# Attention of the first two batches turned on TensorE, first loads in a fixed order on two queues, folded weights of the second batch from slices that are still on the chip

## The chip, the cores and the metric

The kernel runs on one core of a Trainium2 chip. The metric is device time in microseconds (us): the median of the runs of the program, of which there are three for the kernel before. A profiled execution of the same program gives the trace; its own time is told beside its span. TensorE is called PE in the rows (its weight loads PEld), VectorE is DVE, ScalarE is ACT, GpSimd is POOL, SyncE is SP.

## The reference

For 8 batches of 8 heads, 576 tokens and a head size of 64, with 32 memory slots per head:

```
a    = softmax(phi over the tokens)            # phi: 576 x 32 per head
k_m  = a^T k ; v_m = a^T v                     # 32 x 64 per head
attn = softmax(q k_m^T / sqrt(64)) v_m         # per token over 32 slots
x    = attn with the heads side by side        # 4608 tokens x 512
out  = relu(x w_in)^2 w_out                    # 512 -> 2048 -> 512
```

w_in and w_out come as 64-bit floats; q, k, v and phi as 32-bit floats.

## The kernel before

**Folding.** The kernel never forms x. For each batch it multiplies v_m into w_in once (the folded weights, tile `vw`, 2048 columns in 8 slices of 256) and then multiplies the attention weights (tile `ath` and its rest `atl`) with `vw`. Every product of 32-bit accuracy is made of three products of a high and a low part, which is why tiles come in pairs (`ath`/`atl`, `gh`/`glo`, `VTh`/`VTl`).

**Stages.** `memory(b, hh)` (hh is one half of the heads) takes the softmax of phi (tiles `phi`, `mx`, `mc`, `pmx`) and multiplies it with k and v (tile `pkv`, lines L426 and L439). `scores` and `attention` turn q by blocks of 32x32 on VectorE (L546), multiply it with the block-diagonal k_m (`kb`, L539; product L551), turn the scores back on VectorE (L555), take the softmax over slots (L563 to L570) and turn the result once more on VectorE (L585) into `ath` and `atl`. `piece` and `decode` load a slice of w_in or w_out as 64-bit words (`raw`, L322) and make two 32-bit parts of it on VectorE, ScalarE and partly TensorE (L324 to L357); for w_out slices from the third on, the last sum is an accumulating DMA from POOL (L361). `vw_alone` folds a slice for the first two batches (L493, L501), `vw_step` for the others. `step(g)` is one batch times one block of 128 of the 2048 columns: `mm1` (L622, relu and square), `mm2` (L652, L653, L655 into the four banks `acc`). There are 128 such steps.

**Order.** Batch 0 takes the first 8 column blocks, then batch 1 those 8 and the other 8, then batch 0 its other 8; the batches behind come one by one. Every decoded w_in slice is written to DRAM (L364, two DMAs of 256 KB per half slice, from POOL) and read again later (`wi_again`, L369): for slices 0 to 3 already for the second batch, for all slices again for batches 2 to 7.

**Who sets the order.** The code only records operations with their reads and writes. `Plan.order` then lists them by planned costs and due times and issues each engine's instructions in that one order; an engine carries out its list strictly in order, so whatever stands behind a waiting instruction waits with it. Nearly all loads are issued by SP.

Of the kernel before, what the change touches and what calls it, by code (L numbers as in the profile page):

```python
# [26 lines left out]
LANDS = {"SP": 1400, "POOL": 4000}  # L27
# [179 lines left out]
def tile_attention_moe(  # L207
# [54 lines left out]
    def dma(fn, size, r=(), w=(), eng="SP", two=False, **more):  # L262
        e = {"SP": nc.sync, "POOL": nc.gpsimd}[eng]
        issue = 700 if eng == "POOL" else 1250 if two else 620
        return op({eng: issue}, lambda _: fn(e.dma_start), r=r, w=w, size=size, lat=0, **more)
# [19 lines left out]


# [9 lines left out]
    w_in_parts = []  # L296
    for x in ("hi", "lo"):
        t = dram.tile([DM, FF], F32, name=f"w_in_{x}")
        w_in_parts.append(plan.buf(f"w_in_{x}", lambda _, t=t: t))
    wi = {}  # L300
    wo = {}

    def wi_rows(x, s, hh):

        return w_in_parts[x]()[2 * hh * P:(2 * hh + 2) * P, s * SL:(s + 1) * SL].rearrange("(c p) f -> p c f", p=P)

    def decode(kind, j, h, room):
# [14 lines left out]
        dma(lambda d: d(R().rearrange("p (c f t) -> p c f t", c=src.shape[1], t=2), src), 4096 * P, w=[rk], lead=True)  # L322
# [6 lines left out]
        if kind == "wi":  # L329
            t = wi[0, j, 0, h] = st([P, 2, 2, SL], F32R, "wi", f"wi0_{j}_{h}", 3)  # L330
# [31 lines left out]
        if kind == "wi":  # L362
            for x in (0, 1):
                dma(lambda d, x=x: d(wi_rows(x, j, h), t()[:, x].bitcast(F32)), 2048 * P, r=[(t, (h, x))], w=[(w_in_parts[x], (j, h))], eng="POOL", lead=True)  # L364

    def wi_again(n, s, hh):
        t = wi[n, s, 1, hh] = st([P, 2, 2, SL], F32R, "wi", f"wi{n}_{s}_{hh}", 3)
        for x in (0, 1):
            dma(lambda d, x=x: d(t()[:, x].bitcast(F32), wi_rows(x, s, hh)), 2048 * P, r=[(w_in_parts[x], (s, hh))], w=[(t, (hh, x))], lead=True)  # L369
# [22 lines left out]
    def memory(b, hh, where=None):  # L392
# [5 lines left out]
        dma(lambda d: tokens(d, a(), phi[b, 4 * hh:4 * hh + 4]), 4 * S * M * 4, [], [(A, "in")], two=True, lead=True)  # L398
        KV = []
        for x in (0, 1):  # L400
            t = st([P, 4 * SC * D], F32, where[x] if where else "KV", f"KV{u}_{x}", 1 if where else 2)
            kv = lambda t=t: t().rearrange("p (i h c d) -> p i h c d", i=2, h=2, c=SC)
            for i, src in ((0, k), (1, v)):
                dma(lambda d, i=i, src=src, kv=kv, x=x: tokens(d, kv()[:, i], src[b, 4 * hh + 2 * x:4 * hh + 2 * x + 2]),
                    2 * S * D * 4, [], [(t, i)], two=True, lead=True)
# [28 lines left out]
        def sums(e):  # L434
# [49 lines left out]
    def vw_alone(s, bp):  # L484

        ts_ = [wi[0, s, bp if s < 4 else 0, hh] for hh in (0, 1)]
# [17 lines left out]
    def vw_step(n, s, hh):  # L504
        t = wi[n, s, 1, hh]
# [22 lines left out]
    def scores(b, hh, split):  # L528
# [284 lines left out]
```

## Time and profile before

| | |
|---|---|
| three runs | 831.05 us median, 829.07 to 832.75 |
| the profiled execution | 829.28 us, of which the span is 827.6 us |
| granted TensorE clock, mean over the span | 0.983 of 2.4 GHz |
| TensorE busy | 777.8 us, 94% of the span |
| VectorE busy | 547.2 us, 66% |
| ScalarE busy | 396.4 us, 48% |
| moved by DMA | 101.05 MB |

The busy share of TensorE is an average over stages that differ: in the first 60 us it is idle for 24 us, from 250 us to 810 us for 2 us. The span has to be read stage by stage. Matmuls are pipelined and their ends are modelled, so a busy TensorE is not always one at its peak; where its granted clock is 0.5 it is at 1.2 GHz, otherwise at 2.4 GHz.

### The profile page before, as it was taken

How to read it: one execution, taken by the hardware profiler on the slowest of the kernel's cores; microseconds unless marked ns; L12 is line 12 of the kernel's file. 1: busy time of each engine (PE TensorE's matmuls, PEld its weight loads, DVE VectorE, ACT ScalarE, POOL GpSimd, SP SyncE). 2: the span in 40 equal slices, each digit the busy share in tenths (PEclk: the TensorE clock that was granted, in tenths of full speed). 3: DMA queues.
4: the chain of work that ended last, by engine and by line, in shares of the span. 5: the costliest groups of instructions: out<-in, count | busy, mean ns of one | idle time of the engine just before them, and what ended most of it. 6: DMA issues, size and time to landing. Idle time of an engine off the chain costs nothing.

```text
span 827.6 us, 13055 instructions
## 1 busy us (share of the span) xinstructions
PE 777.8 (94%) x4820; PEld 650.1 (79%) x4820; DVE 547.2 (66%) x1224; ACT 396.4 (48%) x904; POOL 65.1 (8%) x103
## 2 busy tenths in 40 slices
PE   4679998899979999999999999999999999999995
PEld 2346887788868788888788888888788888888883
DVE  3888997484447856786768465786778555874540
ACT  1456676476535355554436355453434355543220
POOL 3112211221100100001000100010000100000000
PEclk9999999899999999999999999999999999999998
DMA  7978956566455543322562433413512433100001
GB/s 213 292 223 274 264 162 180 158 186 187 112 147 165 146 129 103 102 55 54 141 171 58 126 115 103 124 38 96 140 45 79 130 109 97 40 19 33 1 1 63
DMA packets 92804, 101.05 MB, mean 122 GB/s; under 512 B 24836, under 2 KB 78084, under 8 KB 92740
## 3 DMA queue, kind: packets, MB, share of 16 engines
q1 hardware_dynamic: 80292, 81.55, 34.1%
q0 software_dynamic: 12448, 18.66, 9.3%
q8 instruction: 38, 0.62, 0.3%
q14 instruction: 26, 0.21, 0.1%
HBM read 79.17 MB, written 17.83 MB: 117 GB/s over the span
## 4 chain that ended last, share of the span: by engine, by line
PE 69%; DVE 11%; DMA 9%; issue 4%; ACT 4%; SPq 1%; POOL 1%; DVEq 0%; ACTq 0%; POOLq 0%
PE h L622 19%; PE acc L655 12%; PE acc L652 11%; PE acc L653 11%; PE accl L678 5%; PE pvw L513 4%; DMA raw<-in_moe_w_in_dram 3%; PE psc L551 2%; PE pkv L426 2%; DMA wo<-work 2%; DMA phi<-in_phi_dram 2%; ACT vw L260 1%; DMA q<-in_q_dram 1%; DMA raw<-in_moe_w_out_dram 1%; DVE glo L632 1%
## 5 line engine op out<-in xcount | busy, mean ns | idle before, releaser
L622 PE MATMUL h<-ath,vw 128*128 128x320 f32 (+1 forms) x1024 | 211.9, 299 | 1.5 <-DVE ath L260 1.3
L652 PE MATMUL acc<-wo,gh 128*128 128x512 f32 x512 | 206.8, 404 | 0.6 <-ACT gh L628 0.4
L653 PE MATMUL acc<-wo,gh 128*128 128x512 f32 x512 | 202.1, 395 | 0.0
L622 PEld LDWEIGHTS h<-ath,vw 128*128 128x128 f32 x1024 | 172.1, 190 | 18.2 <-DVE ath L260 1.9
L655 PE MATMUL acc<-wo,glo 128*128 128x512 f32 x512 | 163.7, 412 | 3.5 <-DVE glo L632 3.3
L260 ACT CAST vw<-pvw 64x256 fp32r<-64x256 f32 (+1 forms) x224 | 85.8, 397 | 94.5 <-PE pvw L513 47.1
L522 DVE TENSOR_TENSOR vw<-pvw,vw 64x256 fp32r<-64x256 f32 x192 | 78.7, 420 | 73.5 <-ACT vw L260 71.7
L652 PEld LDWEIGHTS acc<-wo,gh 128*128 128x128 f32 x512 | 96.8, 189 | 21.0 <-issue 2.2
L622 PE MATMUL h<-atl,vw 128*128 128x320 f32 (+1 forms) x512 | 110.7, 296 | 0.2
L655 PEld LDWEIGHTS acc<-wo,glo 128*128 128x128 f32 x512 | 91.0, 191 | 24.1 <-DVE glo L632 10.1
L653 PEld LDWEIGHTS acc<-wo,gh 128*128 128x128 f32 x512 | 96.8, 189 | 16.5
L628 ACT ACTIVATE gh<-r 128x512 fp32r<-128x512 f32 x128 | 80.7, 630 | 41.8 <-DVE r L627 30.4
L632 DVE TENSOR_TENSOR glo<-r,gh 128x512 fp32r<-128x512 f32 x128 | 87.5, 684 | 12.1 <-ACT r L630 10.0
L626 ACT ACTIVATE r<-h 128x256 f32<-128x256 f32 (+1 forms) x146 | 58.8, 405 | 64.9 <-PE h L622 63.8
L627 DVE TENSOR_SCALAR r<-h 128x320 f32<-128x320 f32 (+1 forms) x110 | 50.3, 459 | 56.3 <-PE h L622 55.7
L622 PEld LDWEIGHTS h<-atl,vw 128*128 128x128 f32 x512 | 83.1, 191 | 1.2 <-DVE atl L589 0.8
L630 ACT ACTIVATE r<-r 128x576 f32<-128x576 f32 x99 | 67.8, 685 | 2.4
L629 ACT ACTIVATE gl<-r 128x64 fp32r<-128x64 f32 x128 | 32.6, 255 | 64.1 <-DVE r L627 62.1
L678 PE MATMUL accl<-wo,gl 128*128 128x512 f32 x192 | 52.3, 396 | 0.1
L678 PEld LDWEIGHTS accl<-wo,gl 128*128 128x128 f32 x192 | 34.9, 188 | 7.3 <-DVE o L260 0.5
L551 PE MATMUL psc<-qT,kb 128*128 128x256 f32 (+1 forms) x128 | 37.8, 415 | 1.6 <-DVE S L555 1.4
L513 PE MATMUL pvw<-wi,VTh 128*128 128x256 f32 x192 | 37.6, 288 | 0.3 <-DVE vw L522 0.3
(107 smaller groups left out, 836.0 us busy)
## 6 DMA issues: line engine op xcount, KB each, us to landing
wi<-w_in_hi SPq DMA_DIRECT2D x56, 256.0 KB
wi<-w_in_lo SPq DMA_DIRECT2D x56, 256.0 KB
q<-in_q_dram SPq DMA_DIRECT2D x32, 288.0 KB
KV<-in_k_dram SPq DMA_DIRECT2D x32, 256.0 KB
KV<-in_v_dram SPq DMA_DIRECT2D x32, 256.0 KB
raw<-in_moe_w_in_dram SPq DMA_DIRECT2D x16, 512.0 KB
raw<-in_moe_w_out_dram SPq DMA_DIRECT2D x16, 512.0 KB
out_dram<-o POOLq DMA_DIRECT2D x20, 256.0 KB, 8.3
```

Source lines behind the costliest of these rows:

```text
L260: nc.scalar.copy(o, i) if e == "ACT" else ENG[e].tensor_copy(o, i)
L513: nc.tensor.matmul(pw()[:, x * SL:(x + 1) * SL], l()[:, 2 * hh + x, :], w(r, x), start=(i == 0), stop=(i == 2))
L522: vec({"DVE": tt(SL)}, lambda e, V=V, pr=pr, src=src: nc.vector.tensor_sub(V()[pr, 1, hh, :], src(), V()[pr, 0, hh, :].bitcast(F32)), [pw, ...
L622: nc.tensor.matmul(p()[:, 0:n], V()[:, l, hh, c0:c0 + P], x()[:, hh, cs], start=(i == 0), stop=(i == 5))
L626: op({"ACT": act(n) - 30, **({} if b < 2 else {"DVE": tt(n)})}, lambda e, cs=cs, n=n, p=p: nc.scalar.activation(r()[:, cs], p()[:, 0:n], A ...
L628: op({"ACT": act(SM)}, lambda e: nc.scalar.activation(gh(), r()[:, 0:SM], AF.Square), [r], [gh])
L630: op({"ACT": act(S), **({} if b < 2 else {"DVE": tt(S)})}, lambda e: nc.scalar.activation(r(), r(), AF.Square) if e == "ACT" else nc.vecto ...
L632: vec({"DVE": tt(SM)}, lambda e: nc.vector.tensor_sub(glo(), r()[:, 0:SM], gh().bitcast(F32)), [r, gh], [glo])
L652: nc.tensor.matmul(a(), gh()[:, c], t()[:, 0], start=f0, stop=False)
L653: nc.tensor.matmul(a(), gh()[:, c], t()[:, 1], start=False, stop=False)
L655: nc.tensor.matmul(a(), glo()[:, c], t()[:, 0], start=False, stop=f1)
L678: nc.tensor.matmul(a(), G()[:, l, :], t()[:, w], start=(ff == 0 and n == 0), stop=(ff == NFF - 1 and n == 2))
```

## The change

1. **First loads.** `dma` may take a name out of a list `FIRST`. Such a load may be issued by SP or by ACT, whichever is free by the plan, and the list fixes the order.
2. **Attention of batches 0 and 1** is a function of its own. q is loaded in natural order (64 values of a token at a time, 256 bytes), turned by TensorE (`turn`, four transposes of 128x128 into a bank), copied by ScalarE, multiplied token block by token block (`psc`: 8 matmuls of 128x64 per half instead of 4 of 128x256 and 128x320), and the softmax result is turned by TensorE again (`back`). k_m and v_m leave `memory` by one pair of TensorE transposes. The 32x32 transposes of VectorE for these two batches are gone; batches 2 to 7 keep them.
3. **The second batch's folded weights.** Slices 0 and 1 of w_in stay in tiles of their own (`W4a` to `W5b`) until batch 1 has used them; slices 2 and 3 are folded for batch 1 directly behind batch 0. The second batch's 16 reads of 256 KB (L369, slices 0 to 3) are gone. `memory(1, *)` and `attention(1)` stand earlier in the program.
4. **The stored slices** lie in DRAM as one tensor in the order of the tile: one DMA of 512 KB per half slice in place of two, for the writes and for the reads that stay (batches 2 to 7).

```diff
-    def dma(fn, size, r=(), w=(), eng="SP", two=False, **more):
-        e = {"SP": nc.sync, "POOL": nc.gpsimd}[eng]
+    def dma(fn, size, r=(), w=(), eng="SP", two=False, first=None, **more):
+        q_ = {"SP": nc.sync, "ACT": nc.scalar, "POOL": nc.gpsimd}
         issue = 700 if eng == "POOL" else 1250 if two else 620
+        ways = {eng: issue}
+        if first in FIRST:
+            ways = {"SP": issue, "ACT": issue}
+            more["cap"] = 10000 * FIRST.index(first) - 1e6
...
+    FIRST = ["phi 0 0", "kv 0 0", "phi 0 1", "wi 0", "q 0 0", "kv 0 1", "q 0 1", "ql 0", "wo 0"]
...
+    w_in_t = dram.tile([NSL, 2, P, 4 * SL], F32, name="w_in_parts")
...
-            t = wi[0, j, 0, h] = st([P, 2, 2, SL], F32R, "wi", f"wi0_{j}_{h}", 3)
+            tag, bufs = ("wi", 3) if j > 1 else (f"W{4 + h}{'ba'[j]}", 1)
+            t = wi[0, j, h] = st([P, 2, 2, SL], F32R, tag, f"wi0_{j}_{h}", bufs)
...
     def wi_again(n, s, hh):
-        t = wi[n, s, 1, hh] = st([P, 2, 2, SL], F32R, "wi", f"wi{n}_{s}_{hh}", 3)
-        for x in (0, 1):
-            dma(lambda d, x=x: d(t()[:, x].bitcast(F32), wi_rows(x, s, hh)), 2048 * P, r=[(w_in_parts[x], (s, hh))], w=[(t, (hh, x))], lead=True)
+        t = wi[n, s, hh] = st([P, 2, 2, SL], F32R, "wi", f"wi{n}_{s}_{hh}", 3)
+        dma(lambda d: d(t().rearrange("p x c f -> p (x c f)").bitcast(F32), w_in_parts()[s, hh]), 4096 * P, r=[(w_in_parts, (s, hh))], w=[t], lead=True)
...
+            def turn_kv(e):
+                for i in (0, 1):
+                    nc.tensor.transpose(pv()[:, i * P:(i + 1) * P], kvx()[:, i].rearrange("p r d -> p (r d)"), ident)
+            op({"PE": 450}, turn_kv, [kvx], [pv], lead=True, lat=300)
+            kbd = kTs[b, hh] = st([P, P], F32, "kb", f"kbd{u}", 2)
...
+    def first_attention(b):
+        bank = lambda name: pt("acc", name, 4) if b == 0 else pt("pa", name)
...
+                    dma(lambda d, hh=hh, Q=Q, h=h: d(Q()[:, :, h * D:(h + 1) * D], q[b, 4 * hh + h, 0:SM].rearrange("(c p) d -> p c d", p=P)),
+                        SM * D * 4, [], [(Q, h)], lead=True, first=f"q {b} {hh}")
...
+                def turn(e, x=x, Q=Q, pq=pq):
+                    for c in range(NMAIN):
+                        nc.tensor.transpose(pq()[:, c * P:(c + 1) * P], Q()[:, c, 2 * x * D:(2 * x + 2) * D], ident)
+                op({"ACT": act(SM)}, lambda e, x=x, qT=qT, pq=pq: nc.scalar.copy(qT()[:, x], pq()), [pq], [(qT, x)], lead=True)
...
+                for c in range(NMAIN):
+                    for x in (0, 1):
+                        nc.tensor.matmul(pc()[:, c * P + 64 * x:c * P + 64 * x + 64], qT()[:, pair(x), c * P:(c + 1) * P],
+                                         kbd()[:, 64 * x:64 * x + 64], start=True, stop=True)
...
+            def back(e, S_=S_, pa=pa):
+                for c in range(NMAIN):
+                    nc.tensor.transpose(pa()[:, c * P:(c + 1) * P], S_()[:, 4 * c:4 * c + 4, :].rearrange("p h m -> p (h m)"), ident)
+            op({"ACT": act(SM)}, lambda e, hh=hh, pa=pa: nc.scalar.copy(ah()[:, hh, 0:SM], pa()), [pa], [(ah, (hh, 0)), (ah, (hh, 1))], lead=True)
...
         piece("wi", j)
         vw_alloc(0, j, (0,))
         vw_alone(j, 0)
+        if j == 2:
+            memory(1, 0)
+            memory(1, 1)
+            attention(1)
+        if j > 1:
+            vw_alloc(0, j, (1,))
+            vw_alone(j, 1)
         piece("wo", j)
         step(2 * j)
         step(2 * j + 1)
-    memory(1, 0)
-    memory(1, 1)
-    attention(1)
     for s in range(4):
-        vw_alloc(0, s, (1,))
-        for hh in (0, 1):
-            wi_again(0, s, hh)
-        vw_alone(s, 1)
+        if s < 2:
+            vw_alloc(0, s, (1,))
+            vw_alone(s, 1)
         step(8 + 2 * s)
```

In the lists below a name holds the tile, then the batch and the half (`q0_1` is q of batch 0, second half of the heads; `qx` its last 64 tokens), then a running number.

**The first loads.** In the kernel before SP issues all of them. This is SP's list from the last k and v load of batch 0 on:

```order
L377 DMA KV0_1_1_143<-in_v_dram 128x2x256
L378 DMA KV0_1_1_143<-in_v_dram 64x2x64
L534 DMA q0_0_168<-in_q_dram 64x1152 x2
L322 DMA raw_184<-in_moe_w_in_dram 128x2x512
L322 DMA raw_190<-in_moe_w_in_dram 128x2x512
L322 DMA raw_196<-in_moe_w_out_dram 128x1024
L377 DMA phi1_0_172<-in_phi_dram 128x4x128
...
L322 DMA raw_276<-in_moe_w_out_dram 128x1024
L377 DMA phi1_1_278<-in_phi_dram 128x4x128
L378 DMA phi1_1_278<-in_phi_dram 64x4x32
L322 DMA raw_293<-in_moe_w_in_dram 128x2x512
L322 DMA raw_308<-in_moe_w_in_dram 128x2x512
L534 DMA q0_1_343<-in_q_dram 64x1152 x2
```

In the changed kernel ACT issues one part. This is ACT's list from the first w_in slice to its first computation on phi (SP has the other half of the same loads at the same places):

```order
L323 DMA raw_105<-in_moe_w_in_dram 128x2x512
L602 DMA q0_0_109<-in_q_dram 128x4x64 x2
L377 DMA KV0_1_0_121<-in_k_dram 128x2x256
L279 ACT_TABLE_LOAD
L279 ACTIVATE minus_68<-ident_63 128x128
L378 DMA KV0_1_0_121<-in_k_dram 64x2x64
L377 DMA KV0_1_1_127<-in_k_dram 128x2x256
L378 DMA KV0_1_1_127<-in_k_dram 64x2x64
L602 DMA q0_1_132<-in_q_dram 128x4x64 x2
L595 DMA qx0_137<-in_q_dram 64x4x64
L323 DMA raw_142<-in_moe_w_out_dram 128x1024
L417 ACTIVATE phi0_0_79<-phi0_0_79 128x640
```

The second half of batch 0's q moved from behind batch 1's first phi, k and v and behind a second w_in slice to directly behind batch 0's own k and v.

**TensorE's first instructions.** Before:

```order
L411 MATMUL pmx0_0_104<-ident_63,mx0_0_97 128x128
L414 MATMUL pmx0_0_104<-ident_63,mc0_0_108 128x128
L439 MATMUL pkv0_0_118<-ones_70,phi0_0_80 32x1 x20
L426 MATMUL pkv0_0_118<-KV0_0_0_86,phi0_0_80 32x128 x2
L426 MATMUL pkv0_0_118<-KV0_0_1_99,phi0_0_80 32x128 x2
```

After:

```order
L411 MATMUL pmx0_0_114<-ident_63,mx0_0_103 128x128
L613 MATMUL pq0_0_0_217<-ident_63,q0_0_109 128x128 x3
L414 MATMUL pmx0_0_114<-ident_63,mc0_0_118 128x128
L613 MATMUL pq0_0_0_217<-ident_63,q0_0_109 128x128
L613 MATMUL pq0_0_1_226<-ident_63,q0_0_109 128x128 x4
L613 MATMUL pq0_1_0_273<-ident_63,q0_1_132 128x128 x4
L613 MATMUL pq0_1_1_284<-ident_63,q0_1_132 128x128 x4
L439 MATMUL pkv0_0_145<-ones_70,phi0_0_79 32x1 x20
```

The products of phi with k and v (`pkv`) now stand behind 16 transposes of q, the last 8 of which need the second half of q.

**The reads of stored slices.** SP's list before, where the second batch's first read stands:

```order
L322 DMA raw_741<-in_moe_w_in_dram 128x2x512
L378 DMA phi2_1_781<-in_phi_dram 64x4x32
L369 DMA wi0_0_0_879<-w_in_hi_78 128x2x256
L369 DMA wi0_0_0_879<-w_in_lo_79 128x2x256
L322 DMA raw_817<-in_moe_w_out_dram 128x1024
L322 DMA raw_847<-in_moe_w_out_dram 128x1024
L534 DMA q1_1_898<-in_q_dram 64x1152 x2
```

After, at the same load of w_in:

```order
L378 DMA phi2_1_773<-in_phi_dram 64x4x32
L323 DMA raw_828<-in_moe_w_in_dram 128x2x512
L323 DMA raw_857<-in_moe_w_in_dram 128x2x512
L323 DMA raw_920<-in_moe_w_out_dram 128x1024
L323 DMA raw_956<-in_moe_w_out_dram 128x1024
L323 DMA raw_995<-in_moe_w_in_dram 128x2x512
```

The loads of 64-bit weights follow one another without reads of stored slices between them.

## Rows read from the trace of the kernel before

**Rows 1.** The page: busy time (share) and instructions, then tenths in 40 slices

```profile
PE 777.8 (94%) x4820; PEld 650.1 (79%) x4820; DVE 547.2 (66%) x1224; ACT 396.4 (48%) x904; POOL 65.1 (8%) x103
...
PE   4679998899979999999999999999999999999995
...
PEclk9999999899999999999999999999999999999998
```

**Rows 2.** Stretches: window, length, busy by engine, granted clock, DMA share, GB/s

```profile
0.00:10.00 10.00, 1.92 (x50) 1.31 (x54) 2.49 (x5) 2.33 (x3) 7.32 (x15) 1.00 0.63 172
10.00:20.00 10.00, 5.68 (x107) 3.80 (x103) 4.55 (x12) 1.26 (x3) 0.20 (x1) 1.00 0.90 245
20.00:30.00 10.00, 7.15 (x37) 3.48 (x26) 8.18 (x22) 3.99 (x9) 2.61 (x4) 1.00 0.97 283
30.00:40.00 10.00, 6.84 (x27) 3.73 (x25) 9.24 (x19) 4.66 (x9) 0.73 (x1) 0.93 0.99 314
40.00:50.00 10.00, 7.05 (x17) 3.82 (x17) 7.69 (x18) 3.88 (x7) 1.82 (x3) 0.73 0.87 247
50.00:60.00 10.00, 7.54 (x106) 5.12 (x106) 9.58 (x23) 6.61 (x13) 1.28 (x3) 1.00 0.71 208
...
90.00:120.00 30.00, 30.00 (x181) 26.86 (x180) 30.00 (x67) 21.41 (x47) 1.85 (x3) 1.00 0.70 195
120.00:130.00 10.00, 7.98 (x45) 6.71 (x43) 4.92 (x11) 5.00 (x11) 3.16 (x4) 1.00 0.90 247
...
150.00:160.00 10.00, 6.02 (x23) 4.90 (x22) 7.12 (x15) 4.19 (x9) 0.78 (x1) 0.73 0.48 138
...
230.00:240.00 10.00, 7.27 (x35) 6.53 (x36) 5.67 (x14) 3.71 (x9) 0.00 (x0) 0.83 0.66 174
...
250.00:810.00 560.00, 558.08 (x3343) 474.41 (x3342) 371.87 (x833) 259.09 (x615) 18.86 (x33) 1.00 0.32 89
```

**Rows 3.** Timeline of the start: start us, duration, instruction, idle before it

```profile
9.76 2.52 PE L426 MATMUL pkv<-KV,phi 128*32 128x128 f32 x40
...
58.68 0.28 PE L622 MATMUL h<-ath,vw 128*128 128x256 f32 x1
...
65.63 0.39 PE L652 MATMUL acc<-wo,gh 128*128 128x512 f32 x1
```

**Rows 4.** Groups by form, 0 to 260 us: xcount | busy, mean ns

```profile
L260 ACT CAST vw<-pvw 128x512 fp32r<-128x512 f32 x32 | 18.7, 583 | 17.4 <-PE pvw L493 16.5 <-PE pvw L501 0.8
...
L350 PE MATMUL pd<-work,ident 128*128 128x512 f32 x24 | 15.4, 725 | 4.9 <-DVE work L327 2.2 <-DVE rz_None L568 1.9 <-ACT vw L260 0.7
...
L551 PEld LDWEIGHTS psc<-qT,kb 128*128 128x128 f32 x36 | 7.1, 204 | 3.7 <-DVE S L555 1.7 <-PE pd L352 0.4 <-issue 0.2
...
L551 PE MATMUL psc<-qT,kb 128*128 128x256 f32 x20 | 6.0, 418 | 0.1
L551 PE MATMUL psc<-qT,kb 128*128 128x320 f32 x16 | 5.1, 439 | 1.3 <-DVE S L555 1.3
...
L564 DVE TENSOR_TENSOR S<-S,red_None 128x576 f32<-128x576 f32 x4 | 3.0, 754 | 0.0
...
L411 PE MATMUL pmx<-ident,mx 128*128 128x128 f32 x8 | 2.7, 337 | 7.0 <-DVE par L284 6.0 <-DVE VTl L471 1.0
```

**Rows 5.** VectorE's waits, 60 to 220 us: us in total, times, longest

```profile
DVE work L324 <- DMA raw<-in_moe_w_in_dram: 6.9, 3, 4.7
DVE work L324 <- DMA wo<-work: 5.3, 1, 5.3
```

**Rows 6.** DMA issues of 60 to 170 us: KB each

```profile
wi<-w_in_hi SPq DMA_DIRECT2D x8, 256.0 KB
wi<-w_in_lo SPq DMA_DIRECT2D x8, 256.0 KB
```

**Rows 7.** TensorE's waits, 60 to 260 us

```profile
PE pvw L501 <- ACT vw L260: 4.3, 2, 4.0
...
PE acc L655 <- DVE glo L632: 3.1, 2, 2.5
```

More of the change, by code (lines that the diff above doesn't have):

```diff
@@ L26 @@
 STEP = 5200
-LANDS = {"SP": 1400, "POOL": 4000}
+LANDS = {"SP": 1400, "ACT": 1400, "POOL": 4000}
 WIRE = 240.0
@@ L260, in copy @@
         nc.scalar.copy(o, i) if e == "ACT" else ENG[e].tensor_copy(o, i)
-    def dma(fn, size, r=(), w=(), eng="SP", two=False, **more):
-        e = {"SP": nc.sync, "POOL": nc.gpsimd}[eng]
+    def dma(fn, size, r=(), w=(), eng="SP", two=False, first=None, **more):
+        q_ = {"SP": nc.sync, "ACT": nc.scalar, "POOL": nc.gpsimd}
         issue = 700 if eng == "POOL" else 1250 if two else 620
-        return op({eng: issue}, lambda _: fn(e.dma_start), r=r, w=w, size=size, lat=0, **more)
+        ways = {eng: issue}
+        if first in FIRST:
+            ways = {"SP": issue, "ACT": issue}
+            more["cap"] = 10000 * FIRST.index(first) - 1e6
+        return op(ways, lambda e: fn(q_[e].dma_start), r=r, w=w, size=size, lat=0, **more)
     def vec(ways, fn, r, w, port=BOTH, **more):
@@ L397, in memory @@
         op({"POOL": 200}, lambda e: nc.gpsimd.memset(a()[LEFT:P, :, NMAIN], -3e38), [], [(A, "pad")], lead=True)
-        dma(lambda d: tokens(d, a(), phi[b, 4 * hh:4 * hh + 4]), 4 * S * M * 4, [], [(A, "in")], two=True, lead=True)
+        dma(lambda d: tokens(d, a(), phi[b, 4 * hh:4 * hh + 4]), 4 * S * M * 4, [], [(A, "in")], two=True, lead=True, first=f"phi {b} {hh}")
         KV = []
@@ L404, in memory @@
                 dma(lambda d, i=i, src=src, kv=kv, x=x: tokens(d, kv()[:, i], src[b, 4 * hh + 2 * x:4 * hh + 2 * x + 2]),
-                    2 * S * D * 4, [], [(t, i)], two=True, lead=True)
+                    2 * S * D * 4, [], [(t, i)], two=True, lead=True, first=f"kv {b} {hh}")
             KV.append((t, kv))
@@ L484, in vw_alone @@
     def vw_alone(s, bp):
-        ts_ = [wi[0, s, bp if s < 4 else 0, hh] for hh in (0, 1)]
+        ts_ = [wi[0, s, hh] for hh in (0, 1)]
         vh, vl = VT[bp]
@@ L702, in store @@
             def store(d, j=j, b=b, c=c):
-                rows = out[b * S:(b + 1) * S, :].rearrange("(p c) e -> c p e", c=NC)
-                d(rows[c:c + n], o()[32 * j:32 * (j + n), :])
+                rows = out[b * S:(b + 1) * S, :]
+                if b > 1:
+                    rows = rows.rearrange("(p c) e -> c p e", c=NC)[c:c + n]
+                elif n == 4:
+                    rows = rows[32 * c:32 * (c + n)]
+                else:
+                    rows = rows[SM:S]
+                d(rows, o()[32 * j:32 * (j + n), :])
             dma(store, 32 * n * DM * 4, [home], [], eng="SP" if b >= B - 2 else "POOL")
```

121 lines of the change are left out of this document (97 added, 24 removed).

## Prediction

> **What bounds the kernel now.** I read the page first: TensorE is busy for 94% of the span, and the slices show where it is not, in the first three (60 us) and at a few dents up to the twelfth [rows 1]. Then the stretches [rows 2]. From 250 to 810 us TensorE is idle for 560.00 - 558.08 = 1.9 us: behind 250 us only less TensorE work would shorten the program. Before 60 us it is idle for 60 - (1.92 + 5.68 + 7.15 + 6.84 + 7.05 + 7.54) = 23.8 us, and its busy time there holds slow matmuls too: the granted clock is 0.73 in 40 to 50 us. Further idle time stands in 120 to 130 us (2.0), 150 to 160 (4.0, clock 0.73) and 230 to 240 (2.7, clock 0.83). Since steps that are ready pile up in front of TensorE later, a microsecond won before 250 us is won at the end, and one that TensorE works more in a full stretch is lost.
>
> The start is bound by loads first and then by a chain. The DMA engines are 90 to 99% busy from 10 to 40 us [rows 2]; 9 MB stand in SP's list up to the second half of batch 0's q. The first steps' matmuls begin at 58.68 us, and the first product with w_out at 65.63 us [rows 3]; from there on TensorE has work.
>
> The dents behind it come from waits of VectorE, which carries out its list in order: 6.9 us in three waits for a w_in slice (longest 4.7) and 5.3 us in one wait for an accumulating DMA of w_out [rows 5]. What TensorE then waits for is what stood behind: 2.5 us for `glo`, 4.0 us for the copy of `vw` [rows 7].
>
> **First loads and first attention.** Up to the second half of q the new list has phi 2 x 288 KB, k and v 2 x 1152 KB, w_in 1024 KB and q 2 x 512 KB, together 4.93 thousand KB or 5.05 MB. In the first 10 us the engines moved 172 GB/s at a share of 0.63, behind that 245 to 283 [rows 2]. With 2 us before the first byte, 5.05 MB at 283 end at 19.8 us and at 245 at 22.6; with 172 GB/s for the first 10 us and 245 behind they end at 23.6. I take 21.5.
>
> The Trainium skill, in "DMA: Bandwidth & Descriptors", section "Issuing engines are not separate DMA queues", says that loads issued from two engines run on the same 16 DMA engines and that only issue time is saved. The trace can bound that: by the share of 0.63 at most 3.7 of the first 10 us [rows 2]. By the rule the order of the loads is the larger part, as in the sum here.
>
> From there the chain is `pkv` of the first half, scores, softmax; then the second half. TensorE's list puts `pkv` behind the transposes of all of q, so it starts at 21.5 instead of about 9 us. One `pkv` takes 0.8 + 2.5 us [rows 3]. I follow the three lists with durations of rows 4. `pkv` ends at 24.8; the division, two VectorE operations, two decode operations that stand between, the transposes and a copy: 2.3, so 27.1; the split of a decoded w_in half by TensorE 1.3 and the scores 1.6: 30. A copy (0.6), the maximum of the second half, its subtraction and exponential: 3.5, so the second `pkv` runs 33.5 to 36.5. VectorE then has a softmax pass of the first half (0.75), the next batch's maximum (1.25), a decode operation and the division: 40.5. Transposes, copies, scores of the second half: 43.5. Its softmax is four passes of about 0.8 on VectorE and one on ScalarE, 4.6 with the small ones, and nine decode operations between them are some 5.4: 53.5. Transposes back and copies: 54.5. The last such copy ended at about 62 us before, and the first w_out product came 3.5 us later. So that product comes at about 60 instead of 65.6: **-5.5 us**. Batch 0's extra TensorE work is in this chain already and otherwise hidden by the idle 23.8 us. Bounds: with loads at 19.8 and half of the decode operations out of the way -10; with loads at 23.6 and 5 us of waiting between the three lists +2.
>
> **Batch 1's attention on TensorE.** This stands in full stretches (30.00 of 30 us busy, 90 to 120 us [rows 2]), so its net TensorE work counts in full. Removed: 16 passes of L551 per batch; 36 passes were busy for 6.0 + 5.1 = 11.1 us [rows 4], so 4.9. Added: 27 + 2 transposes. None of 128x128 in a row is shown: a quarter of a 512-column pass of L350 (15.4 us / 24 / 4) is 0.16, a single transpose is 0.337 in L411 [rows 4], so 4.6 to 9.8. Added further: 40 passes of 64 columns. A quarter of the 256-column L551 pass (6.0 / 20 / 4) is 0.075, its weight load 0.204 [rows 4], so 3.0 to 8.2. Net +2.7 to +13.1. Transposes in a row are pipelined, so I am near the low ends: 4.6 + 4.3 - 4.9 = **+4**. ScalarE gets four copies of 512 columns more at 0.58 [rows 4] and three of scores, about 4 us in a stretch where it is busy 21.41 of 30 us: hidden by slack there, unless a copy comes late for the single bank `pa` that all these products pass through. Then TensorE waits for a copy, 0.6 each, 11 uses: up to 6.4 us more; other work stands between the uses in TensorE's list, so I take 0.
>
> VectorE loses its block transposes, some 8 us per batch. Between 90 and 120 us it is 100% busy, but so is TensorE: no gain by itself, only fewer late decode operations.
>
> **Second batch's slices.** Gone are 16 reads of 256 KB between 60 and 170 us [rows 6], 4.2 MB; at 247 GB/s (120 to 130 us) 17 us of the DMA engines, and 16 issues in SP's list ahead of loads that VectorE waits for. The 4.7 us wait at 120 us stands at a DMA share of 0.90 [rows 2, 5] and cost TensorE 2.0 us there. The accumulating DMA of 150 us stays, but fewer POOL writes stand before it; it cost 4.0 us and some half-clock time. Of the late loads I take all of those 2 us and 1 us of half clock, of the accumulation's 4 us and its half clock a third, 2 us: **-5**. Bounds: both gone, with their half-clock time, -11; a new wait of the same length as the one at 150 us, since slices 2 and 3 now hold the three `wi` tiles until batch 1's v_m is there, +5. The dent at 230 us is a load of a later batch; those lists are alike before and after: 0. The stored slices' DMAs are halved in number, in stretches where TensorE is full: 0, both ways 1 us.
>
> **Sum.** -5.5 + 4 - 5 = -6.5. The profiled execution took 829.28 us (span 827.6, 1.7 outside), which gives 822.8; the median of the runs lies 1.8 above it, so the forecast stands between 822.8 and 824.6: **824 us**, 0.8% faster.
>
> **Rivals.** (a) *More is won*: the chain ends 9 us earlier, and both dents go (-11) against +4: -16, 813. For it: VectorE was 92 to 96% busy from 30 to 40 and 50 to 60 us [rows 2] and loses 8 us there. Against: the new chain runs through three engines and each list holds decode work between.
>
> (b) *Hidden anyway*: the start wins 2, the dents 3, TensorE pays 5: 829 to 831. For it: a dent often moves on to the next late load. Against: the wire is relieved of 4.2 MB in just this stretch.
>
> (c) *Slower, by the order of TensorE's list*: `pkv` waits for the second half of q. The chain from that load to the first w_out product was 60 - 21.5 = 38.5 us above; the start is later than before if the load lands after 65.6 - 38.5 = 27 us. At 172 GB/s throughout [rows 2] it lands at 29.4 + 2 = 31.4, the first product at 70: +4; with +4 for batch 1 and nothing won at the dents 829.3 + 8 = 837. For it: ACT issues 18 loads before its first exponential, and both lists start with small packets, as the first 10 us had. Against: SP's single list was what kept that stretch at 0.63.
>
> (d) *Clock*: in 40 to 50 us the clock was half for a part, behind 30 us in which TensorE had been busy 5.7 to 7.2 of 10 us [rows 2]. If it is granted 1.2 GHz from 22 to 55 us, TensorE's 12 us in the chain cost up to 9 more and eat the start: -5.5 + 9 + 4 - 5 = +2.5, 832. The Trainium skill, in "TensorE: Matmul & The Clock Gate", section "Part 4: PE-mode transpose", says that transposes do not count as TensorE activity for the clock; by that rule the new start would rather see it. No row here shows transposes alone.
>
> **Chances.** Forecast 0.36, (a) 0.22, (b) 0.18, (c) 0.17, (d) 0.07. The forecast's own range is 818 to 829, its last part within 0.5%. About 0.5% (4.2 us) is what a measurement of this kernel tells from no change: faster is below 826.9, slower above 835.2. Faster: 0.22 and nearly all of 0.36: 0.56. Slower: (c) and a rest of (d): 0.18. Same: 0.26. The range takes in most of (a) and (c): 809 to 837.
>
> **What would show it.** Right: the first w_out product at 58 to 62 us, second half of q landed before 24 us, VectorE's waits for w_in under 3 us between 60 and 170 us, the 250 to 810 us stretch as full as before and TensorE's busy sum some 4 to 9 us higher in work of the first two batches. Wrong: `pkv` starting after 27 us, TensorE waiting for ScalarE's copies at the transposes of batch 1, or a new wait of the fold of slices 2 and 3.

## The result, and the profile after

The changed kernel took 833.97 us (median of 20 runs, 831.71 to 839.68), the kernel before 830.29 (20 runs): a ratio of 1.005 with a 95% interval of 1.0028 to 1.0072. It is slower by half a per cent, where 0.8% faster was forecast.

The page of the changed kernel, to be read against [rows 1]:

```profile
PE 782.6 (94%) x4926; PEld 659.9 (79%) x4926; DVE 535.6 (64%) x1189; ACT 402.2 (48%) x923; POOL 50.1 (6%) x87
...
PE   1798999899999999999999999999999999999995
...
PEclk9979999999999999999999999999999999999998
```

The span is 831.1 us. TensorE is busy 4.8 us longer (782.6 against 777.8) and idle 1.3 us less (48.5 against 49.8): +3.5, the difference of the spans. The added work is there, near what was forecast; the idle time that was to pay for it hardly shrank. The stretches say where it stayed (columns as in [rows 2]):

```profile
0.00:10.00 10.00, 0.45 (x1) 0.18 (x1) 1.30 (x2) 0.00 (x0) 7.32 (x15) 1.00 0.82 204
10.00:20.00 10.00, 2.17 (x9) 1.65 (x9) 3.76 (x8) 1.73 (x3) 0.00 (x0) 1.00 1.11 300
20.00:30.00 10.00, 8.78 (x97) 5.79 (x98) 4.80 (x13) 4.91 (x11) 0.26 (x2) 1.00 0.95 257
30.00:40.00 10.00, 6.39 (x112) 4.97 (x110) 8.54 (x21) 5.50 (x12) 1.48 (x3) 0.95 0.99 315
40.00:50.00 10.00, 8.58 (x36) 7.23 (x36) 5.39 (x15) 3.91 (x11) 0.00 (x0) 0.50 0.34 106
50.00:60.00 10.00, 9.21 (x102) 5.18 (x101) 8.72 (x19) 5.55 (x11) 0.20 (x1) 0.87 0.30 89
...
90.00:120.00 30.00, 28.05 (x184) 24.00 (x182) 23.76 (x50) 20.67 (x43) 3.36 (x5) 1.00 0.59 175
120.00:130.00 10.00, 9.27 (x54) 7.62 (x53) 7.75 (x17) 7.40 (x17) 1.44 (x2) 1.00 0.57 164
150.00:160.00 10.00, 6.84 (x32) 5.84 (x31) 7.14 (x15) 4.76 (x10) 0.00 (x0) 0.83 0.42 129
...
160.00:200.00 40.00, 37.69 (x214) 33.07 (x214) 29.46 (x62) 28.18 (x60) 7.23 (x9) 0.96 0.58 169
...
250.00:810.00 560.00, 557.89 (x3387) 475.95 (x3385) 375.56 (x844) 260.30 (x620) 18.45 (x34) 1.00 0.31 91
```

The loads are faster (300 GB/s in 10 to 20 us, 245 before), but TensorE is idle 24.4 us of the first 60, as before (23.8). Its busy time in 40 to 60 us is slow work: the granted clock is 0.50 and 0.87, the lower of the two levels (1.2 GHz) for most of it. By this column twice the missing share of the clock is the time at that level: 1.0 + 10.0 + 2.6 = 13.6 us in the first 60, where before had 1.4 + 5.4 = 6.8. (The column does not show the lower level of the first instructions; see the last section.) At the same time the DMA engines run dry (0.34 and 0.30, before 0.87 and 0.71). The dents of [rows 2] shrank: at 120 us by 1.3 and at 150 by 0.8. Others opened: 1.95 us in 90 to 120, which was full, and 1.95 in 160 to 200 (37.69; before 39.64).

The start on TensorE (timeline, columns as in [rows 3]):

```profile
14.45 0.87 PE L613 MATMUL pq<-ident,q 128*128 128x128 f32 x3 [7.27 <-DMA q<-in_q_dram]
...
20.99 2.03 PE L613 MATMUL pq<-ident,q 128*128 128x128 f32 x8 [4.37 <-DMA q<-in_q_dram]
...
23.69 2.52 PE L426 MATMUL pkv<-KV,phi 128*32 128x128 f32 x40
31.10 1.89 PE L636 MATMUL psc<-kbd,qT 128*128 128x64 f32 x16
...
36.45 1.43 PE L426 MATMUL pkv<-KV,phi 128*32 128x128 f32 x40
43.39 3.51 PE L636 MATMUL psc<-kbd,qT 128*128 128x64 f32 x16
...
64.19 0.40 PE L770 MATMUL acc<-wo,gh 128*128 128x512 f32 x1
```

The second half of q is there at 20.99 us, and `pkv` follows its transposes at 22.9 (9.0 before). The first product with w_out comes at 64.19 us, 1.4 earlier than in [rows 3], not 5.6. The second half's scores take 3.51 us at the lower clock where the first half's took 1.89. On ScalarE (timeline; ACTq rows are DMA issues):

```profile
8.19 2.24 ACTq L602 DMA_DIRECT2D q<-in_q_dram  x2
...
19.87 0.74 ACT L417 ACTIVATE phi<-phi 128x640 f32<-128x640 f32 x1 [7.24 <-DMA q<-in_q_dram]
```

The first exponential ran at 8.2 us before. How much of the delay is ScalarE's own, VectorE's list tells, which makes its operand (the last line is of the kernel before):

```profile
11.54 0.43 DVE L325 TENSOR_SCALAR work<-raw 128x512 f32<-128x512 f32 x1 [4.94 <-DMA raw<-in_moe_w_in_dram]
...
13.35 0.28 DVE L413 TENSOR_REDUCE mc<-pmx 128x1 f32<-128x128 f32 x1
...
15.58 0.82 DVE L415 TENSOR_TENSOR phi<-phi,pmx 128x640 f32<-128x640 f32 x1 [0.80 <-PE pmx L414]
...
7.36 0.82 DVE L415 TENSOR_TENSOR phi<-phi,pmx 128x640 f32<-128x640 f32 x1 [0.57 <-PE pmx L414]
```

The operand is ready at 16.4 us in place of 8.2: the maximum (`mc`) stands behind decode operations that wait for a w_in slice, and `pmx` on TensorE behind transposes that wait for q's first half. From 16.4 to 19.87 the exponential waits for ScalarE's issues, 3.5 us. It ends at 20.6, and `pkv` still waits 2.3 us for q's transposes. So three engines' lists share the delay of `pkv`.

VectorE's waits, 60 to 220 us, to be read against [rows 5] (the last line is of the kernel before):

```profile
DVE work L325 <- DMA raw<-in_moe_w_in_dram: 8.7, 6, 3.9
DVE work L325 <- DMA wo<-work: 7.6, 3, 3.4
DVE work L325 <- DMA raw<-in_moe_w_out_dram: 7.3, 4, 3.5
...
DVE work L324 <- DMA raw<-in_moe_w_out_dram: 2.0, 3, 1.0
```

For the weights VectorE now waits 23.6 us in place of 14.2 (6.9, 5.3 and 2.0). (A wait of 8.7 us for q, which it turned itself before, is gone.)

### The profile page after: what moved, and what is told of

The parts are those of the page before. It is cut to its first block, busy times and chain, and to the rows that moved or that the text cites. A ratio compares the mean times of both kernels' runs of the same rounds, so it can differ in the third digit from the quotient of the medians.

```text
span 831.1 us, 13128 instructions
## 1 busy us (share of the span) xinstructions
PE 782.6 (94%) x4926; PEld 659.9 (79%) x4926; DVE 535.6 (64%) x1189; ACT 402.2 (48%) x923; POOL 50.1 (6%) x87
## 4 chain that ended last, share of the span: by engine, by line
PE 73%; DMA 8%; issue 6%; DVE 6%; ACT 3%; SPq 2%; POOL 1%; DVEq 0%; POOLq 0%; ACTq 0%
PE h L740 19%; PE acc L773 12%; PE acc L770 12%; PE acc L771 11%; PE accl L796 5%; PE pvw L536 4%; PE psc L574 2%; PE pkv L426 2%; DMA wo<-work 2%; DMA raw<-in_moe_w_in_dram 2%; DMA phi<-in_phi_dram 2%; DMA KV<-in_v_dram 1%; SPq L378 1%; PE pvw L516 1%; PE pd L352 1%
## 5 line engine op out<-in xcount | busy, mean ns | idle before, releaser
L773 PE MATMUL acc<-wo,glo 128*128 128x512 f32 x512 | 161.7, 406 | 2.4 <-DVE glo L750 2.2
L748 ACT ACTIVATE r<-r 128x576 f32<-128x576 f32 x94 | 64.4, 685 | 2.2
L749 DVE TENSOR_TENSOR r<-r 128x576 f32<-128x576 f32 x34 | 25.7, 757 | 15.8 <-ACT gh L746 14.5
```

The source lines that it names most:

```text
L748: op({"ACT": act(S), **({} if b < 2 else {"DVE": tt(S)})}, lambda e: nc.scalar.activation(r(), r(), AF.Square) if e == "ACT" else nc.vecto ...
L773: nc.tensor.matmul(a(), glo()[:, c], t()[:, 0], start=False, stop=f1)
```

## The experiments

Ratios are to the kernel before, measured beside each; medians are of 6 to 12 runs, of 20 for the changed kernel. Every edit lets the planner order all lists anew, so a run differs from its neighbour in more than the line that is shown. First all runs in one table; columns: loads that ScalarE issues ahead of its first exponential (17 by the trace of the changed kernel; the prediction and the expectations count 18), start of that exponential, start of `pkv`, time at the lower clock in the first 60 us by the clock column, median, ratio with its interval. For the first four runs there were two theories: TensorE's added work eats what the start wins (1), or the fixed first loads themselves cost (2).

| run | issues | exp | pkv | low clock | us | ratio |
|---|---|---|---|---|---|---|
| before | 0 | 8.2 | 9.0 | 6.8 | 830 | 1 |
| after | 17 | 19.9 | 22.9 | 13.7 | 833.97 | 1.005 [1.0028, 1.0072] |
| e1_reuse_alone | 0 | 8.3 | 9.1 | 6.8 | 825.59 | 0.993 [0.9903, 0.9958] |
| e2_reuse_and_first | 12 | 18.8 | 19.6 | 17.1 | 841.54 | 1.0104 [1.0056, 1.0153] |
| e3_no_first | 0 | 8.6 | 9.4 | 3.4 | 818.45 | 0.9853 [0.9801, 0.9904] |
| e4_batch0_on_pe | 17 | 20.5 | 23.0 | 17.1 | 840.07 | 1.0106 [1.0062, 1.0149] |
| f1_order_one_queue | 0 | 8.2 | 9.0 | 3.4 | 819.74 | 0.9869 [0.9818, 0.992] |
| f2_two_queues_no_order | 12 | 16.2 | 18.4 | 20.5 | 826.75 | 0.9934 [0.9898, 0.9969] |
| f3_two_queues_first_half | 6 | 15.1 | 17.8 | 0 | 818.46 | 0.9846 [0.9801, 0.9892] |
| f4_second_q_by_gpsimd | 17 | 20.0 | 23.5 | 23.9 | 838.05 | 1.0089 [1.0058, 1.0119] |
| g1_gap_filled | 17 | 20.3 | 22.5 | 10.2 | 827.55 | 0.9972 [0.994, 1.0005] |
| g2_busy_from_start | 18 | 30.8 | 32.4 | 30.7 | 838.16 | 1.0099 [1.0071, 1.0126] |
| g3_scalar_issues_seven | 6 | 14.9 | 15.7 | 3.4 | 821.08 | 0.9898 [0.9849, 0.9948] |
| g4_scalar_issues_eleven | 11 | 14.0 | 14.8 | 0 | 812.9 | 0.9784 [0.9733, 0.9835] |
| h1_pkv_between | 13 | 16.8 | 17.6 | 17.1 | 824.81 | 0.9942 [0.9913, 0.997] |
| h2_kv_ahead_of_q | 17 | 20.5 | 23.3 | 13.7 | 832.98 | 1.0023 [0.9991, 1.0056] |

**The parts apart.** e1 and e3 leave the fixed first loads out, e1 and e2 put all attention back on VectorE (in e2 the old load of q takes part in the fixed order), e4 batch 1's alone:

```
-        if b < 2:                      (memory, attention, store)
+        if b in BY_PE:                 e1, e2: ()   e4: (0,)
-    FIRST = ["phi 0 0", "kv 0 0", ...]
+    FIRST = []                         e1, e3
```

> Parts 3 and 4 alone (slices of the second batch used from the chip, stored slices as one tensor); attention of all batches on VectorE, all first loads by SP in the planner's order. Theory 1 (the change pays with TensorE work for what the removed reads win): 2 to 5 us faster than the kernel before, TensorE's busy sum as before (778 us). Theory 2 (the fixed first loads are what costs): the same, 2 to 5 us faster. Theory 3 (slices 2 and 3 hold the wi tiles until the second batch is ready and stall the decode): 2 or more us slower than before.

> Parts 1, 3 and 4 without part 2: the fixed first loads on two queues, attention of all batches on VectorE. Theory 1: at least as fast as e1, up to 4 us faster, since the second half of q comes 15 us or more earlier and no TensorE work is added. Theory 2: 2 to 5 us slower than e1, since ACT issues loads and the loads of the second batch come late.

> The changed kernel without part 1: TensorE turns the first two batches' attention, all loads by SP in the planner's order. Theory 1: 1 to 4 us slower than the changed kernel (835 to 838), TensorE's busy sum as in the changed kernel (782). Theory 2: 2 to 5 us faster than the changed kernel (829 to 832).

> The changed kernel with the second batch's attention back on VectorE; the first batch's stays on TensorE. Theory 1: TensorE does about 3.5 us less in full stretches, so 2 to 4 us faster than the changed kernel (830 to 832). Theory 2: within 1.5 us of the changed kernel.

The reuse of the slices alone wins 5 us (e1). TensorE's attention on top of it wins another 7 (e3 against e1); with batch 1's share back on VectorE the kernel is 6 us slower by the medians and 4.6 by the ratios (e4 against after), which neither theory expected. The fixed first loads cost 15.5 us (after against e3), and 16 without TensorE's attention (e2 against e1). Theory 1 falls: the part that was to win loses more than the others gain. Theory 2 had the direction right and the size wrong: it expected 2 to 5 us. In e3 the start went as hoped for:

```profile
10.12 2.52 PE L426 MATMUL pkv<-KV,phi 128*32 128x128 f32 x40
...
57.50 0.39 PE L770 MATMUL acc<-wo,gh 128*128 128x512 f32 x1
```

**Order, queues, late loads.** f1 keeps the order and drops the second queue, f2 the reverse; f3 keeps both for the first half's phi, k and v alone; f4 takes the second batch's q out of SyncE's list:

```
+            ways = {"SP": issue}                       f1 (was "SP" and "ACT")
-            more["cap"] = 10000 * FIRST.index(first) - 1e6     f2
+    FIRST = ["phi 0 0", "kv 0 0"]                      f3
+    ... first=f"q {b} {hh}", eng="POOL" if b else "SP")        f4
```

> The changed kernel with the fixed order of the first loads kept, but every load issued by SyncE: ScalarE issues none of them. The first half's k and v sums (pkv) stand ahead of q's transposes in TensorE's list again. Three theories of the 15 us that the first loads cost. Order of TensorE's list and ScalarE's issues (both come from the second queue here): the first pkv starts at 10 to 13 us, ScalarE's first exponential before 12 us, the first product with w_out comes at 57 to 60 us, and the time is 818 to 824. Order of the loads alone (q ahead of the second half's k and v): 828 to 834, with a first product at 62 us or later. Late loads of the second batch and of the weights: 826 to 832, the wire idle around 50 us as in the changed kernel.

> The changed kernel with the two queues kept for the first loads, but without the fixed order: they are issued as they fall due. TensorE's list has one quarter of q's transposes ahead of the first pkv. If the two queues are what costs (issues in ScalarE's list, and what then stands ahead of pkv): 829 to 836, first pkv behind 18 us, first product with w_out at 63 us or later. If the fixed order is what costs: 817 to 824, with that product at 57 to 60 us. If late loads of the second batch decide: 824 to 832 with raw w_in waits of VectorE over 5 us before 130 us.

> The changed kernel with two queues and the fixed order for phi, k and v of the first half alone; q, the second half and the weights go as they fall due, by SyncE. ScalarE issues 6 loads instead of 18 ahead of its first exponential. If issuing from ScalarE as such costs, about 822 to 826 (a third of the 15 us); if the order of what comes behind costs, 815 to 820, as with no fixed first loads at all (818.45), the first pkv at 8 to 12 us and the first product with w_out at 55 to 59 us.

> The changed kernel with the ten loads of the second batch's q issued by GpSimd, so that in SyncE's list nothing waits for the buffers of the first q ahead of the second batch's phi, k, v and the next w_in slices. TensorE's list is the same up to the first steps. If the late loads behind that wait are a main part of the 15 us: the w_in slices are issued 5 us or more earlier, VectorE's raw w_in waits between 60 and 130 us shrink from 8.7 us to under 4, and the time is 824 to 829; the first product with w_out stays at 63 to 65 us. If the order of the first half's chain decides alone: 831 to 835.

The order alone costs nothing (f1), nor does a second queue for the first half's phi, k and v (f3, though its `pkv` starts at 17.8 us, where 8 to 12 was expected). Two queues for all nine names without the order cost about half, 8 us against e3 (f2); it has the time that the theory of late loads expected, and 10.6 us of VectorE's waits for w_in before 130 us (6.5 in e3). f4 leaves its question open: it is 4 us slower still and outside both of its ranges, but in its list SyncE then waits up to 8.3 us for the buffers of k and v (released by `pkv`), and the w_in slice that the changed kernel issues at 36.32 us is issued at 41.03, not earlier. f1's start, the earliest of all:

```profile
9.73 2.52 PE L426 MATMUL pkv<-KV,phi 128*32 128x128 f32 x40
...
51.30 0.50 PE L770 MATMUL acc<-wo,gh 128*128 128x512 f32 x1
```

Its first product is 6.2 us ahead of e3's, its time is no better. And f3 starts `pkv` 8 us later than e3 with the same time. So neither the start of `pkv` up to 18 us nor the first product decides alone. f2 and f3 start `pkv` within 0.6 us of each other and differ by 8 us, and by 20.5 us of lower clock; with the clock the stalls differ too, so this pair does not separate them. f3's stretches:

```profile
40.00:50.00 10.00, 8.88 (x109) 5.50 (x107) 10.00 (x24) 6.59 (x12) 0.73 (x2) 1.00 0.82 235
50.00:60.00 10.00, 10.00 (x57) 8.23 (x55) 6.48 (x17) 7.12 (x16) 0.53 (x1) 1.00 0.66 204
```

With a full clock TensorE and VectorE are both at work and the loads go on, where the changed kernel has 0.50 and 0.34.

**The clock, and ScalarE's list.** g1 and g2 add matmuls of ident by ident, which nothing reads, in the gap between the transposes of q's halves (g1) and at the head of TensorE's list (g2); g3 and g4 shorten the list of loads that ScalarE shares:

```
+    for i in range(16): op({"PE": 10}, beat, [], [(pq, i)], ...)    g1
+    for i in range(4):  op({"PE": 10}, go, [], [beat], ...)         g2, 14 matmuls each
+    ways = {"SP": issue, "ACT": issue} if FIRST.index(first) < 3 else {"SP": issue}   g3
+    FIRST = ["phi 0 0", "kv 0 0", "phi 0 1", "kv 0 1", "wi 0"]      g4
```

> The changed kernel with 16 more matmuls of 128 columns (ident by ident, overwritten later) in TensorE's list, 15 of them between the transposes of q's first and second half, where TensorE waited 4.4 us for a load; the lists are otherwise the same up to there. If the half clock that the changed kernel had from 38.4 to 52.1 us comes from TensorE being idle in the first 21 us (2.2 us busy in 10 to 20), the half clock is gone or under 5 us long, the first product with w_out comes 4 to 7 us earlier (57 to 60 us), and the time falls by 5 to 10, to 824 to 829. If the clock is only a follower of the late start, it stays 10 us or longer, and the time is 832 to 836.

> The changed kernel with 56 more matmuls of 128 columns (ident by ident, overwritten later) at the head of TensorE's list, some 15 us of work that ends near 17 us; the first pkv then stands ahead of the second half of q's transposes, and ScalarE's first exponential two copies and a load later in its list. Clock theory: no half clock between 30 and 60 us, 822 to 830 even though q's first transposes start 2 to 3 us later. Other theory (late start alone): the half clock shorter or not, 833 to 838.

> The changed kernel with the fixed order kept, but only the loads of the first three names (phi and v of the first half, the second phi) shared with ScalarE, which issues 6 instead of 18 ahead of its first exponential; the others by SyncE. In TensorE's list pkv stands behind one of q's transposes instead of sixteen. If ScalarE's long list of issues is what costs (through the late exponential, pkv and clock): first exponential at 14 to 16 us, no half clock over 4 us before 60, first product with w_out at 52 to 58 us, 817 to 823. If the order of the loads costs with two queues: 828 to 834.

> The changed kernel with the fixed order and the two queues for phi, k, v and the first w_in slice alone; q and w_out by SyncE as they fall due. ScalarE issues 11 loads ahead of its first exponential instead of 18, and pkv stands ahead of q's transposes. If the cost grows with ScalarE's issues and the order of TensorE's list together: first exponential at 15 to 17 us, first product with w_out at 54 to 62 us, 818 to 827. If two queues cost nothing as long as pkv stands ahead of q's transposes: 817 to 821 without a half clock over 4 us before 60.

g1 fills an idle gap and wins 6.4 us against the changed kernel. Its lists are nearly those of the changed kernel up to 38 us; behind that the planner ordered them otherwise. Its timeline (the 15 fillers of the gap stand as 30 rows):

```profile
16.61 4.59 PE L613 MATMUL pq<-ident 128*128 128x128 f32 x30
21.09 0.63 PE L617 MATMUL pq<-ident,q 128*128 128x128 f32 x4
21.94 0.63 PE L617 MATMUL pq<-ident,q 128*128 128x128 f32 x4 [0.22 <-DMA q<-in_q_dram]
...
23.02 1.43 PE L426 MATMUL pkv<-KV,phi 128*32 128x128 f32 x40
```

The eight transposes that took 2.03 us now take 1.26, and the 40 passes of `pkv` 1.43 instead of 2.52: the filler brought TensorE to its higher level earlier. In the profiled executions the 4926 instructions of the program itself took 774.4 us on TensorE, in place of 782.6; without its fillers TensorE was idle for 47.9 us, in place of 48.6. So g1's gain is work done faster, not a wait that is gone. The stretch at the lower one fell to 10.2 us only, where under 5 had been expected. g2 shows the other half: busy for 8.27 of the first 10 us, then idle, TensorE was at the lower level from 20 to 30 us, and the start was the latest of all:

```profile
0.00:10.00 10.00, 8.27 (x61) 8.28 (x62) 1.33 (x2) 0.00 (x0) 7.31 (x15) 1.00 0.85 217
...
20.00:30.00 10.00, 3.98 (x9) 2.11 (x10) 7.88 (x16) 4.79 (x8) 0.00 (x0) 0.50 0.56 176
```

So g2 missed its expectation: its list has the exponential behind still more (30.8 us), and says little on the clock theory. g3 and g4 take the cost away. g4, with two queues for all but q and w_out, is the fastest kernel of the study, 2.2% faster than before and better than both ranges expected, with 1.00 in the clock column in every stretch of the first 60 us:

```profile
30.00:40.00 10.00, 9.01 (x137) 7.61 (x136) 6.60 (x15) 4.87 (x12) 0.29 (x2) 1.00 0.97 302
40.00:50.00 10.00, 8.42 (x104) 4.53 (x103) 8.88 (x20) 6.89 (x14) 0.91 (x1) 1.00 0.70 186
```

**Which place in the lists.** h1 ranks the first exponential ahead of everything, which puts `pkv` between the transposes of q's halves and the exponential ahead of four of the issues; h2 is g4 with q and w_out shared too, behind the second half's k and v:

```
+  op({"ACT": act(640)}, ... AF.Exp ..., cap=-2e6 if u == "0_0" else None)    h1
+  FIRST = ["phi 0 0", "kv 0 0", "phi 0 1", "kv 0 1", "wi 0", "q 0 0", "q 0 1", "ql 0", "wo 0"]   h2
```

> The changed kernel with the first exponential ranked ahead of everything in the planner: in ScalarE's list it stands three loads earlier (15 issues ahead of it instead of 18), and in TensorE's list pkv stands between the transposes of q's two halves instead of behind both. Loads, queues and their order are otherwise those of the changed kernel. If TensorE's list (pkv behind the second half of q) is the main cause: pkv starts by 20 us, TensorE is busy 4 us or more from 10 to 20, the half clock before 60 us is under 7 us, and the time is 820 to 827. If ScalarE's issues ahead of the exponential are the main cause, little changes: exponential at 17 to 20 us, half clock over 10 us, 829 to 835.

> The changed kernel with all nine names in the fixed order and shared by both queues, but the second half's k and v ahead of q. Against the run with eleven issues by ScalarE (812.9) its first 11 issues are the same; then come q's and w_out's ahead of the first exponential, and TensorE's list has q's transposes ahead of pkv. If these two places in the lists are the cause: first exponential behind 18 us, pkv behind the transposes of q, half clock over 10 us before 60, first product with w_out at 62 us or later, 828 to 836. If k and v behind q was the cause: 813 to 820.

h1 wins 9 us against the changed kernel, with `pkv` at 17.6 instead of 22.9 us. Its lower clock was expected to shorten and grew to 17.1 us, and TensorE's busy sum stayed (781.9 us, 782.6 in the changed kernel) while its idle time fell by 6.1 us: what h1 won is not the clock's. The exponential comes 3.0 us earlier too, so h1 does not separate the two lists. h2 has g4's first eleven issues in ScalarE's list, then the six of q and w_out, and costs 20 us more, as expected in every mark. On ScalarE:

```profile
13.35 5.38 ACTq L602 DMA_DIRECT2D q<-in_q_dram  x4
...
20.46 0.74 ACT L417 ACTIVATE phi<-phi 128x640 f32<-128x640 f32 x1 [6.85 <-DMA q<-in_q_dram]
```

and on VectorE the step that the exponential waits for:

```profile
12.02 0.81 DVE L415 TENSOR_TENSOR phi<-phi,pmx 128x640 f32<-128x640 f32 x1
```

The exponential could have run at 12.8 us and ran at 20.46, because six DMA issues stood ahead of it in the same list. Most of that time is not issuing. The row of 5.38 us holds four issues of 0.37 to 0.49 us, at 13.35, 14.78, 17.79 and 18.23; between them ScalarE waits. By the trace's record of semaphores, the first loads of both queues take eight semaphores in turn, and each load from the ninth on waits, before it is issued, until the load that used its semaphore last has landed. The one at 17.79 us starts 0.02 us after the w_in slice that SyncE issued at 12.41 has landed. So ScalarE's list stands still until an earlier load is through, also one of the other queue. In the changed kernel the gaps in front of ScalarE's 17 issues add up to 8 us, nearly as much as the issues themselves (9.1 us). In g4, with its operand ready at 13.0, the exponential runs at 14.04:

```profile
14.04 0.72 ACT L417 ACTIVATE phi<-phi 128x640 f32<-128x640 f32 x1
```

## Why the prediction was wrong

**The step that failed** is the first term, "First loads and first attention", -5.5: it let `pkv` start 12 us later at no cost, and it read the start by its first product alone. Measured, the main part of the term, the fixed loads on two queues, costs 15.5 us (after against e3). The load itself was read rightly: q's second half was forecast for 21.5 us and is used at 20.99. From there the chain slipped step by step: first `pkv` ends at 26.2 (24.8 forecast), first scores at 33.0 (30), second `pkv` at 37.9 (36.5), second scores at 46.9 (43.5), first product at 64.19 (60). That is 4 us late, and still earlier than before; the rest of the loss lies behind it. The changed kernel, then e3:

```profile
0.00:60.00 60.00, 35.57 (x355) 24.99 (x355) 32.51 (x75) 21.59 (x44) 9.26 (x20) 0.89 0.75 212
60.00:250.00 190.00, 177.71 (x1140) 149.99 (x1139) 126.05 (x271) 119.58 (x261) 22.43 (x33) 0.98 0.57 169
...
0.00:60.00 60.00, 40.55 (x396) 27.35 (x397) 34.64 (x80) 25.36 (x51) 10.31 (x22) 0.97 0.81 237
60.00:250.00 190.00, 184.75 (x1256) 155.71 (x1255) 136.03 (x294) 123.59 (x269) 21.58 (x33) 0.99 0.58 171
...
PE 778.9 (95%) x4926; PEld 654.7 (80%) x4926; DVE 536.3 (66%) x1197; ACT 400.8 (49%) x915; POOL 49.9 (6%) x87
```

Both run the same 4926 instructions on TensorE. Against e3, whose span is 815.7 us, TensorE is idle 5.0 us more in the first 60 us and 7.0 more from 60 to 250, and its work takes 3.7 us longer (782.6 against 778.9); behind 250 us it is idle 0.2 less. Together that is the difference of the spans. Three things hang on it.

*ScalarE's issues as work in ScalarE's list.* They were named only as a sign of slow loads, in rival (c). In fact they hold back the exponential, by 3.5 us in the changed kernel and by 7.6 in h2. The Trainium skill, in "DMA: Bandwidth & Descriptors", section "Issuing engines are not separate DMA queues", says that starting DMAs from several engines saves only the issue time. The trace agrees (in the first 30 us the changed kernel moved 7.6 MB, f1 with one queue 7.2), and shows the other side of it: the issues, and the waits in front of them, are then spent by an engine on which the chain waits.

*The place of `pkv` behind q's transposes.* The forecast had it, and rival (c) let it cost only if q landed after 27 us. It costs already at 21: moved ahead of the second half's transposes, together with the exponential, it wins 9 us (h1). By their times (d), 832, and (c), 837, lie nearest to the 834 measured; that is luck, since (c)'s load was to land at 31 us and (d)'s half clock was to last from 22 to 55 us (13.6 us by the column).

*The clock.* Rival (d), with a chance of 0.07, put a price of up to 9 us on it. g1 gives 6.4 back. The causes are not additive: h1 won 9 us with a longer stretch at the lower clock. How the 12 us of idle time divide between the lists of ScalarE, TensorE and VectorE and the loads that come late behind them is open. What the runs show is the switch: with q and w_out left to SyncE as they fall due the cost is gone (g4), with them in the order on both queues it is back (h2, 20 us).

**"A microsecond won before 250 us is won at the end"** does not hold for the first product: f1 and e3 differ by 6.2 us in it and not in time. A likely reason is the decoding of the weights, which feeds the steps behind: of TensorE's 48 decode products (`pd`), 40 had started by 90 us in the changed kernel, and all 48 before, in e3 and in f1. No run changes the decoding alone, so this is argued, not shown.

**Batch 1's attention on TensorE** was sized rightly as work, +4. Eight rows of the timeline hold its main part, of which three stand here:

```profile
86.77 0.60 PE L613 MATMUL pq<-ident,q 128*128 128x128 f32 x4
...
98.66 1.89 PE L636 MATMUL psc<-kbd,qT 128*128 128x64 f32 x16
...
115.76 0.60 PE L664 MATMUL pat<-ident,S 128*128 128x128 f32 x4
```

Transposes are six groups of four at 0.60 to 0.66, scores two of 1.89. With the leftover rows that is 8.7, and the 16 passes removed were 4.6 in four rows of before (1.10, 1.24, 1.03, 1.24): net +4.1. TensorE waited 0.29 us for a copy of ScalarE's, once. But the sign on the time was wrong: in all, batch 1's attention on TensorE wins 5 to 6 us (e4 against after). That VectorE's 8 us, costed at nothing "by itself", are what outweighs TensorE's 4 is likely; no run changes one without the other.

**The second batch's slices** were right in sum: -5 forecast, -5.0 measured (e1, with the stored slices as one tensor). The split was not: in e1 TensorE is busy 0.9 us more in 120 to 130 us (2 forecast) and 3.4 more in 150 to 160, and 2.1 less in 160 to 200. In the changed kernel the dents at 120, 150 and 230 us shrank, but others opened: VectorE waits 8.5 us for w_in between 60 and 170 us, where under 3 was the mark.

**More is won**, rival (a), has the time of another version: g4 took 812.9 us, (a) says 813. In part that is luck: g4's first product is 9.4 us earlier than before, as (a) has it, but the dents stayed (TensorE busy 7.66 us in 120 to 130, 7.13 in 150 to 160).

## What to carry to other kernels

A DMA issue on a compute engine is an instruction in that engine's list: count what stands behind it and what it waits for itself, above all in the first microseconds, where a chain starts. When a scheduler sets the lists, moving a load forward also moves its consumer forward, past work that was ready earlier; read the order of the consumer before the arrival of the load is priced. An early milestone (the first product here) is no measure of the end: compare idle and busy time of the full engine stage by stage. Relief of an engine that is not the bottleneck (VectorE here) is to be priced by an experiment, not put at nothing.

## What was not expected of the hardware

The granted clock in the profile's stretches is 1.00 from 0 to 30 us, while the same 40 passes took 2.52 us at 9.76 [rows 3] and at 23.69 us after, and 1.43 at 36.45 us, in a stretch at 0.95. The durations tell that TensorE begins at its lower level and rises after it has worked (in g1, behind 4.59 us of filler, the 40 passes took 1.43 us already at 23.02); the clock column shows only the falls behind that. The Trainium skill, in "TensorE: Matmul & The Clock Gate", section "Part 1: The HAM clock gate (the "warmup" mystery)", says that the throttled state is the default and activity releases it; the durations agree, and the column does not.

A load can wait for another before it is issued: with two queues, four loads of q stretch over 5.38 us on ScalarE (h2) with 1.8 us of issuing in them. On one queue SyncE issued eight of them in 4.82 us, one behind the other, in e3:

```profile
16.57 4.82 SPq L602 DMA_DIRECT2D q<-in_q_dram  x8
```
